# Attention kernel on one Trainium2 core: part of the exps moves from ScalarE to VectorE, under a new order of TensorE's queue

## The chip, the core and the metric

The kernel runs on one core of one Trainium2 chip. The metric is the device time of one execution in microseconds (us), the median of several runs. The engines are called as the profile calls them: PE is TensorE (matmuls; PEld its weight loads), ACT is ScalarE, DVE is VectorE, POOL is GpSimd, SP is SyncE, which issues DMAs.

## The reference

Two attentions over the same 2048 tokens of 512 features, mixed by a gate for each token:

```
g = sigmoid((x * gate_w).sum(-1))
a = A(x)    # 32 query heads of 16, one k and one v head that all of them share
b = B(x)    # 32 heads of 16, each with its own k and v
out = g * a + (1 - g) * b
# in both: p = softmax(q k^T / 4), o = p v, then o @ wo
```

There is no mask, so each of the 64 heads has 2048 x 2048 scores, and each score needs one exp.

## The kernel before, in words

The work is laid out as *groups*: 8 of them, attention A and B in turn, 8 heads each (`groups`). A group has two *halves* of 1024 queries; a half has four *banks*, each with 4 heads and 512 queries; a bank walks through 16 chunks of 128 keys. One chunk of one bank is a *quad*: 4 blocks of scores, 128 keys by 512 queries. So there are 64 banks of 16 quads. ACT takes two blocks at a time: one *exp* is one activation on 128 x 1024 scores, two exps make a quad, 32 exps a bank, 2048 exps the kernel.

For exp number `u`, `scores(u)` (matmuls L529, the exp L533) has PE write two blocks of scores into one of two PSUM tiles `sc`, as eight matmuls on 64 x 32 parts of the array. ACT reads them and writes the exps to one of six SBUF tiles `pr`. `values(m, half)` (L548) has PE multiply the exps of quad `m` with v, for 256 of the 512 queries; v carries a column of ones, so sums of exps come along. The results of a bank add up in one pair of PSUM banks `aux`; there are two such pairs. While one pair gathers a bank, the other (`spare()`) serves all else that PE does. At a bank's end `emptied` has DVE read the gathered pair (`raw`, L193 and L194), SP spreads it by DMAs to `dT` and `oT` (L570), and the pairs change their roles.

The rest of PE's work is *units*: the projections of q, k and v of the coming group (12 products each, L189), the turning of v (L416) and the output projections of the heads that are done (3 products, L189). A product is eight matmuls of 512 columns. When a unit's last product is out, DVE reads the spare pair (L193 and L194, or L450 for the output), and only then may the next unit write it. For q and k DVE also clips and splits the result (L356, L201, L202), and POOL's DMA queue lays it out for the scores (L338, eight DMAs to a move, a move at most every six exps). DVE's other work is *side* work: reciprocals (L462) and products (L469 to L471) of the softmax, and checks of the inputs' range (L198).

The program is recorded in order, in one loop over `u`, and each engine runs its instructions in that order. `_Tasks` holds the units and the side work. Its clock counts what PE has been given, in ns: `SCORES` 213 for the scores of an exp, `HALF` 428 for half a quad's values, `PRODUCT` 216 for a product, against `EXP` 916 for an exp of ACT; `busy` counts likewise for DVE. For each `u` the loop records the scores, one or two halves of values, products while they fit before the next exp, and side work while `busy` allows it.

Of the kernel before, what the change touches and what calls it, by code (L numbers as in the profile page):

```python
# [18 lines left out]
P = 128  # L19
# [3 lines left out]
DH = 16  # L23
# [8 lines left out]
FULL = 1500  # L32
LATE = 250
# [8 lines left out]
S_MAX = 40.0  # L42
RANGED = ["x", "gate", "wk_a", "wv_a", "wq_a", "wo_a", "wq_b", "wk_b", "wv_b", "wo_b", "v_a", "v_b"]
# [21 lines left out]
class _Tasks:  # L65
# [4 lines left out]
    def __init__(self):  # L70
        self.now, self.clock, self.busy, self.empty = 0, 0, 0, 0
        self.units, self.open, self.side = [], deque(), deque()
        self.moves, self.moved = deque(), 0

    def add(self, units, after, due, more=0):

        self.units += [(after, due, u, more) for u in units]
        self.units.sort(key=lambda u: u[1])
# [9 lines left out]
    def given(self, ns):  # L88
        self.busy = max(self.busy, self.clock + LATE) + ns

    def product(self, left):

        if not self.open:
            for u in self.units:
                if u[0] <= self.now and self.empty <= self.clock and len(u[2]) + 1 <= left:
                    self.units.remove(u)
                    self.open.extend(u[2])
                    self.more = u[3]
                    break
# [4 lines left out]
        if not self.open:  # L104
            self.given(FULL)
            self.empty = self.busy + LATE
            self.given(self.more)
        return True

    def late(self):  # L110

        n = len(self.open)
        for u in self.units:
            n += len(u[2]) + 3
# [12 lines left out]

    def flush(self):

        assert not self.moves  # L130
# [22 lines left out]
def _fast(ctx, tc, x, wq_a, wk_a, wv_a, wo_a, wqkv_b, wo_b, gate_w, out, flag):  # L153
    nc = tc.nc
    cst = ctx.enter_context(tc.tile_pool(name="cst", bufs=1))
    inp = ctx.enter_context(tc.tile_pool(name="inp", bufs=6))
    wts = ctx.enter_context(tc.tile_pool(name="wts", bufs=2))
    ops = ctx.enter_context(tc.tile_pool(name="ops", bufs=2))
    prob = ctx.enter_context(tc.tile_pool(name="prob", bufs=6))
    ps_s = ctx.enter_context(tc.tile_pool(name="ps_s", bufs=2, space=PSUM))  # L160
# [53 lines left out]
    weights, ready = {}, set()  # L214
    todo = _Tasks()

    def load_w(src, gi, queues=(nc.sync, nc.sync)):
# [4 lines left out]
        def one(part, at, bufs):  # L222
            w = inp.tile([P, BLK], F32, tag="in", name=f"w{part}{src}{gi}")
            w3 = w.rearrange("p (c m) -> p c m", c=NK)
            queues[part == "o"].dma_start(w if part == "o" else w3,
# [11 lines left out]
        if src == "a":  # L237
            one("q", wq_a[:, cols], 2)
            one("o", wo_a[cols, :], 3)
        else:  # L240
            for n, part in ((1, "k"), (2, "v"), (0, "q")):
                one(part, wqkv_b[:, n * D + gi * P : n * D + (gi + 1) * P], 2 if part == "q" else 1)
            one("o", wo_b[cols, :], 3)
# [5 lines left out]
    first_w = load_w("a", 0, (nc.scalar, nc.gpsimd))  # L249
# [40 lines left out]
    def kv_products(b, i, bank):  # L290
# [12 lines left out]
        kn = ops.tile([P, 4, 2, 4, DH], F16, tag="kn", name=f"kn{b}")  # L303
# [23 lines left out]
    def project(w, needs, name, kind, n0, half, parts, put, queues, late=None):  # L327
# [4 lines left out]
        def lay(p):  # L332
# [8 lines left out]
            ready.add((name, half, p))  # L341

        def product(i, c, a, b, first, last):
# [10 lines left out]
            y = ops.tile([P, BLK], F32, tag="y", name=f"y{name}{half}{i}")  # L354
# [36 lines left out]
    def v_units(gi):  # L391
# [3 lines left out]
        def product(b, n):  # L395
# [6 lines left out]
            y = ops.tile([P, BLK], F32, tag="y", name=f"yv{gi}{b}")  # L402
            v16 = ops.tile([P, 2, BLK], F16, tag="v16", name=f"v16{gi}{b}")
# [3 lines left out]
            todo.add([[lambda t=t: turned(b, v16, t) for t in range(4)]], todo.now + 4, todo.now, -400)  # L407

        def turned(b, v16, t):
# [15 lines left out]
            turns[gi] = turns.get(gi, 0) + 1  # L425
            if turns[gi] == 4:
                ready.add(("v", gi))
# [3 lines left out]
    turns = {}  # L431
# [24 lines left out]
    def norm_pieces(src, gi, half, t8, last):  # L456
# [7 lines left out]
        def parts():  # L464
            o, d = oT[src, gi, half, j][:, cols], dT[src, gi, half, j][:, cols]
            if t8 == 0:
                o16s[src, gi, half] = ops.tile([P, 2, 2 * BLK], F16, tag="o16", name=f"o16{src}{gi}{half}", bufs=3)
            o16 = o16s[src, gi, half][:, :, t8 * P : (t8 + 1) * P]
# [4 lines left out]
                     todo.now + (64 if last and half else 300))  # L473
# [44 lines left out]
    probs = {}  # L518

    def scores(u):  # L520
        todays = blocks[ACT * u : ACT * (u + 1)]
        sc = ps_s.tile([P, ACT, BLK], F32, tag="sc", name=f"sc{u}")
        for i, (n, half, _, c, p, j, hh) in enumerate(todays):
# [4 lines left out]
            for a in range(0, P, COLS):  # L528
                nc.tensor.matmul(sc[a : a + COLS, i], k[r, c * P + a : c * P + a + COLS],  # L529
# [290 lines left out]
```

## Time and profile before

| what | value |
|---|---|
| time, median of 3 runs (lowest to highest) | 1957.51 us (1956.01 to 1959.62) |
| the profiled execution's own time | 1959.14 us |
| its span, first to last instruction | 1956.9 us |
| mean granted clock of PE | 0.991 |
| busy: PE, ACT, DVE, POOL | 95%, 97%, 39%, 23% of the span |
| exps on ACT | 2048, from 28.4 us to 1927.2 us |

Busy shares are averages over the span. Instructions of ACT and of PE overlap with the next one, so the time that one takes is longer than the time from its start to the start of the next; where work is counted, the distance between starts is what matters. An idle stretch of an engine is put down to whatever released it last.

### The profile page before, as it was taken

What the parts mean: (1) busy time and instruction counts of PE and PEld (TensorE: products, weight loads), DVE (VectorE), ACT (ScalarE), POOL (GpSimd) and SP (SyncE); (2) the same over time, 40 slices, a digit from 0 to 9 for tenths busy, and PEclk for the clock granted to TensorE, in tenths of its full rate; (3) what the DMA queues carried; (4) which work ended last, traced back from release to release, by engine and by line L of the source; (5) the groups of instructions that cost most, each with busy time, mean ns of one, the idle gap of its engine ahead of it and who ended that gap; (6) DMA issues with size and microseconds to landing.
All of it is one profiled execution on the core that took longest, in us unless ns stands there. A gap on an engine that the chain in (4) does not pass through costs nothing.

```text
span 1956.9 us, 127404 instructions
## 1 busy us (share of the span) xinstructions
PE 1857.9 (95%) x59664; PEld 1060.7 (54%) x59664; DVE 756.9 (39%) x1429; ACT 1895.2 (97%) x2071; POOL 444.7 (23%) x840
## 2 busy tenths in 40 slices
PE   7999999999999999999999999999999999999995
PEld 4555655454555655555455655555455555555442
DVE  5344434343233344424234334443324334443432
ACT  4999999999999999999999999999999999999994
POOL 5344033230054031223034203302303502030000
PEclk8999999999999999999999999999999999999997
DMA  4121011110022010111012101100101201011101
GB/s 143 25 55 36 10 37 34 33 34 15 11 55 49 12 34 19 29 36 33 13 35 42 39 15 31 37 21 25 36 14 32 58 15 25 21 36 31 36 25 42
DMA packets 55736, 65.01 MB, mean 33 GB/s; under 512 B 21440, under 2 KB 29632, under 8 KB 55200
## 3 DMA queue, kind: packets, MB, share of 16 engines
q0 software_dynamic: 24112, 24.89, 6.4%
q1 hardware_dynamic: 30400, 31.46, 6.2%
q8 instruction: 469, 7.68, 1.7%
q14 instruction: 67, 0.55, 0.1%
q10 hardware_dynamic: 688, 0.43, 0.1%
HBM read 10.55 MB, written 4.19 MB: 8 GB/s over the span
## 4 chain that ended last, share of the span: by engine, by line
ACT 83%; issue 8%; PE 7%; DVE 2%; DMA 0%; SPq 0%; POOL 0%; ACTq 0%; DVEq 0%
ACT pr L533 82%; PE aux L548 3%; PE sc L529 2%; PE aux L189 2%; DVE xT L269 0%; DVE acc L450 0%; DMA acc<-in_A_x_dram 0%; PE aux L416 0%; ACT xT L268 0%; DVE dTb L462 0%; PE pt L264 0%; PE aux L297 0%; DMA dTb<-rawb 0%; PE aux L318 0%; PE aux L264 0%
## 5 line engine op out<-in xcount | busy, mean ns | idle before, releaser
L533 ACT ACTIVATE pr<-sc 128x1024 f32<-128x1024 f32 x2048 | 1884.6, 1191 | 12.6 <-PE sc L529 11.7
L548 PE MATMUL aux<-pr,vA 64*32 64x256 f32 x16384 | 685.3, 377 | 2.3 <-issue 1.9
L548 PE MATMUL aux<-pr,vB 64*32 64x256 f32 x16384 | 646.7, 376 | 0.1
L529 PE MATMUL sc<-Qa,kA 64*32 64x512 f16 x8192 | 453.4, 384 | 18.4 <-issue 0.3
L529 PE MATMUL sc<-Qb,K 64*32 64x512 f16 x8192 | 424.1, 385 | 41.8
L529 PEld LDWEIGHTS <-K 64*32 64x32 f16 x8192 | 209.3, 89 | 387.5 <-issue 309.0
L548 PEld LDWEIGHTS aux<-pr,vA 64*32 64x32 f32 x16384 | 335.7, 105 | 58.0 <-issue 15.1
L529 PEld LDWEIGHTS <-kA 64*32 64x32 f16 x8192 | 209.7, 90 | 277.3 <-issue 207.3
L548 PEld LDWEIGHTS aux<-pr,vB 64*32 64x32 f32 x16384 | 309.7, 105 | 35.4 <-issue 0.7
L450 DVE SCALAR_TENSOR_TENSOR acc<-aux,gate_up,acc 128x512 f32<-128x512 f32 x240 | 180.2, 751 | 326.6 <-PE aux L189 312.9
L338 POOL DMA_DIRECT2D Qa<-hia x118 | 57.8, 489 | 449.4 <-PE sc L529 299.1
L338 POOL DMA_DIRECT2D Qb<-hib x128 | 62.3, 486 | 359.5 <-DVE hib L201 181.7
L189 PE MATMUL aux<-w16ob,o16b 64*32 64x512 f16 x1536 | 80.3, 391 | 15.1 <-ACT o16b L470 13.2
L189 PE MATMUL aux<-xT,w16vb 64*32 64x512 f16 x1536 | 93.8, 376 | 0.1
L193 DVE TENSOR_SCALAR rawb<-aux 128x512 f32<-128x512 f32 x32 | 22.1, 689 | 179.9 <-PE aux L548 179.7
L338 POOL DMA_DIRECT2D K<-hik x128 | 61.5, 485 | 109.3 <-DVE hik L201 102.4
L189 PE MATMUL aux<-xT,w16kb 64*32 64x512 f16 x1536 | 82.2, 376 | 0.0
L189 PE MATMUL aux<-xT,w16qb 64*32 64x512 f16 x1536 | 79.9, 376 | 0.0
L189 PE MATMUL aux<-xT,w16qa 64*32 64x512 f16 x1536 | 79.5, 376 | 0.4 <-DVE xT L269 0.2
L189 PE MATMUL aux<-w16oa,o16a 64*32 64x512 f16 x1536 | 79.3, 376 | 0.0
L462 DVE RECIPROCAL dTa<-dTa 128x128 f32<-128x128 f32 x64 | 55.6, 918 | 59.8 <-DMA dTa<-rawa 59.8
L462 DVE RECIPROCAL dTb<-dTb 128x128 f32<-128x128 f32 x64 | 55.4, 916 | 52.9 <-DMA dTb<-rawb 52.9
(135 smaller groups left out, 991.2 us busy)
## 6 DMA issues: line engine op xcount, KB each, us to landing
acc<-in_A_x_dram SPq DMA_DIRECT2D x16, 256.0 KB, 5.9
dTa<-rawa SPq DMA_DIRECT2D x128, 32.0 KB, 2.6
oTa<-rawa SPq DMA_DIRECT2D x128, 32.0 KB, 3.2
K<-hik POOLq DMA_DIRECT2D x128, 32.0 KB, 2.7
K<-lok POOLq DMA_DIRECT2D x128, 32.0 KB, 2.9
Qb<-hib POOLq DMA_DIRECT2D x128, 32.0 KB, 2.5
Qb<-lob POOLq DMA_DIRECT2D x128, 32.0 KB, 2.8
out_dram<-acc SPq DMA_DIRECT2D x16, 256.0 KB, 2.6
```

The costliest lines, as they stand in the source:

```text
L189: nc.tensor.matmul(out[n : n + COLS], lhsT[r, n : n + COLS], rhs[r], start=start, stop=stop)
L193: nc.vector.tensor_scalar(dst, outs[0], scale, None, op0=ALU.mult)
L338: queues[(8 * p + n) % len(queues)].dma_start(op[to : to + DH].rearrange("d (a q) -> d a q", a=2), state[part][rows])
L450: nc.vector.scalar_tensor_tensor(acc[:, t], bank, g, acc[:, t], op0=ALU.mult, op1=ALU.add)
L462: nc.vector.reciprocal(d, d)
L529: nc.tensor.matmul(sc[a : a + COLS, i], k[r, c * P + a : c * P + a + COLS], Q[src, gi, half, p][r, j * BLK : (j + 1) * BLK], start=True, s ...
L533: nc.scalar.activation(probs[u][:, :m], sc[:, :m], AF.Exp, scale=SCALE / (UP * UP))
L548: nc.tensor.matmul(o[32 * i : 32 * i + 32, cols], v[r], probs[at // ACT][r, at % ACT, cols], start=c == half == 0, stop=c == NT - 1 and ha ...
```

## The change

1. **Two exps of some quads are made by DVE.** `choose` may take the last quad of the bank after the one being worked on, if the quad that is being reached is among the first seven of its bank (`LATEST`), the fourth bank has begun, DVE's backlog is short and k and q have been laid. Its two pairs of blocks are left out of ACT's row. Instead each becomes a unit of PE: `vector_scores` writes the scores to the spare `aux` pair. DVE then makes the exps with nine instructions: two that read PSUM and write the score, scaled by 2^23/ln 2 and shifted, as int32; two bitwise ones that part the 23 low bits (as a float near one) from the exponent's bits; and five multiply-adds of a polynomial in the first part, the last of which multiplies with the second, a power of two. All but the first two work on 128 x 1024 in SBUF. The last seven are `fill`: `beside` records them one by one where DVE is expected to have time.
2. **The order follows PE's time.** `slip` and `max(..., todo.clock)` let the planned clock run over an exp's 916 ns, by up to `OVER` 160 before products stop; values of the two kinds of quads are taken as they are expected to be ready; values are recorded without scores between them while more than six exps wait for theirs. So products now come in another pattern: two after one exp and one after the next, where before there was one after each.
3. **Dates and tiles.** v's four units have dates of their own, output units are due before the end (`ends_by`), output weights are loaded later, and `emptied` records all side work that is due (`hurry`) ahead of a bank's reading. To make room, the pool for weights has 3 tiles instead of 6, and `y`, `v16`, `oT` and `dT` one instead of two.

The first rows on ACT around the last quad of bank 34, before; `pr` and `sc` carry the number of the exp:

```order
L533 ACTIVATE pr1116_29253<-sc1116_29244 128x1024
L533 ACTIVATE pr1117_29280<-sc1117_29271 128x1024
L533 ACTIVATE pr1118_29310<-sc1118_29301 128x1024
L533 ACTIVATE pr1119_29352<-sc1119_29343 128x1024
L533 ACTIVATE pr1120_29371<-sc1120_29362 128x1024
```

And the same place in the changed kernel:

```order
L569 ACTIVATE pr1116_29501<-sc1116_29492 128x1024
L569 ACTIVATE pr1117_29520<-sc1117_29511 128x1024
L569 ACTIVATE pr1120_29539<-sc1120_29530 128x1024
L569 ACTIVATE pr1121_29558<-sc1121_29549 128x1024
L569 ACTIVATE pr1122_29588<-sc1122_29579 128x1024
```

Exps 1118 and 1119 are gone from ACT's queue. In the whole program 1974 rows of this kind are left of 2048: 74 exps, the last quads of 37 banks, have moved.

DVE before, where the second q unit for the later half of this group is read (`ya`), and then the bank (`raw`):

```order
L193 TENSOR_SCALAR ya_27583<-aux_82 128x512
L194 SCALAR_TENSOR_TENSOR ya_27583<-aux_83,ya_27583 128x512
L356 TENSOR_SCALAR ya_27583<-ya_27583 128x512
L201 TENSOR_SCALAR hia_26894<-ya_27583 128x512
L202 SCALAR_TENSOR_TENSOR loa_26895<-ya_27583,hia_26894 128x512
L198 TENSOR_REDUCE stats<-ya_27583 128x1
L193 TENSOR_SCALAR rawa_27675<-aux_84 128x512
L194 SCALAR_TENSOR_TENSOR rawa_27675<-aux_85,rawa_27675 128x512
```

DVE in the changed kernel, from the last row of that unit on; `vpr` are the exps that DVE makes, `part` the two bit parts:

```order
L234 TENSOR_REDUCE stats<-ya_28309 128x1
L581 TENSOR_SCALAR vpr_28398<-aux_85 128x512
L581 TENSOR_SCALAR vpr_28398<-aux_86 128x512
L587 TENSOR_SCALAR part_28458<-vpr_28398 128x1024
L587 TENSOR_SCALAR part_28460<-vpr_28398 128x1024
L581 TENSOR_SCALAR vpr_28498<-aux_85 128x512
L581 TENSOR_SCALAR vpr_28498<-aux_86 128x512
L592 SCALAR_TENSOR_TENSOR vpr_28398<-part_28458 128x1024
L485 SCALAR_TENSOR_TENSOR acc<-aux_85,gate_up,acc 128x512
L485 SCALAR_TENSOR_TENSOR acc<-aux_86,gate_up,acc 128x512
L592 SCALAR_TENSOR_TENSOR vpr_28398<-vpr_28398,part_28458 128x1024 x3
L229 TENSOR_SCALAR rawa_28736<-aux_87 128x512
```

Between the unit and the bank's reading now stand the work for two exps, in part, and the reading of an output unit (`acc`); the polynomial of exp 1118 (`vpr_28398`) is cut in pieces by the readings, and three of its steps stand right ahead of the bank's.

PE in the changed kernel, at the scores of exp 1118, between the values of exps 1070 and 1071 and the next scores for ACT:

```order
L613 MATMUL aux10_87<-pr1071_28291,vA_95 32x256
L613 MATMUL aux11_88<-pr1071_28291,vA_95 32x256
L562 LDWEIGHTS kA_94
L562 MATMUL aux00_85<-Qa200_24708,kA_94 32x512
L562 LDWEIGHTS kA_94
L562 MATMUL aux00_85<-Qa200_24708,kA_94 32x512
```

These scores go to an `aux` pair and stand where a product could stand, some 44 exps ahead of their old place; before, all scores went to `sc`.

The core of the diff:

```diff
+NARROW = 710
+LATEST = 6
+WIDE = 1240
+OVER = 160
...
     def given(self, ns):
         self.busy = max(self.busy, self.clock + LATE) + ns
+    def beyond(self, ns):
+        self.busy = max(self.busy, self.begun) + ns
...
-    def beside(self, until):
+    def beside(self, until, urgent):
+        limit = until + (len(self.open) * EXP + 600 if self.open else 1400)
+        def filled():
+            while self.fill and self.busy <= until + EXP and max(self.busy, self.begun) + self.fill[0][1] <= limit:
+                f, ns = self.fill.popleft()
+                f()
+                self.beyond(ns)
+        if urgent:
+            filled()
         while self.side and self.side[0][0] <= self.now and self.busy <= until:
             _, f, ns = self.side.popleft()
             f()
-            self.given(ns)
+            self.beyond(ns)
+        filled()
...
-    inp = ctx.enter_context(tc.tile_pool(name="inp", bufs=6))
+    inp = ctx.enter_context(tc.tile_pool(name="inp", bufs=3))
+    vec = ctx.enter_context(tc.tile_pool(name="vec", bufs=1))
...
+    def vector_scores(u):
+        sc = spare()
+        products(u, sc)
+        asked.remove(u)
+        held[0] += 1
+        probs[u] = pr = vec.tile([P, ACT, BLK], F32, tag="pr", name=f"vpr{u}", bufs=3)
+        fix = pr.bitcast(I32)
+        for i in range(ACT):
+            nc.vector.tensor_scalar(fix[:, i], sc[i], SCALE / (UP * UP) / math.log(2) * 2.0 ** 23, -(2.0 ** 23),
+                                    op0=ALU.mult, op1=ALU.add)
+        parts = []
+        def part(a, b, op):
+            t = vec.tile([P, ACT, BLK], I32, tag=f"part{len(parts)}", name=f"part{len(parts)}{u}")
+            nc.vector.tensor_scalar(t, fix, a, b, op0=ALU.bitwise_and, op1=op)
+            parts.append(t.bitcast(F32))
+        def horner(i):
+            m, power = parts
+            nc.vector.scalar_tensor_tensor(pr, pr if i < 4 else m, VEC[i], m if i else power, op0=ALU.add, op1=ALU.mult)
+            if i == 0 and u % 2:
+                taken[u // 2] = max(todo.busy, todo.begun) + WIDE + LATE
+        todo.fill.append((lambda: part(0x7FFFFF, 125 << 23, ALU.bitwise_or), NARROW))
+        todo.fill.append((lambda: part(0x7F800000, 0x40000000 | VEC5, ALU.bitwise_xor), NARROW))
+        todo.fill.extend((lambda i=i: horner(i), WIDE) for i in range(4, -1, -1))
...
+        todo.hurry()
         raw = ops.tile([P, BLK], F32, tag="raw", name=f"raw{src}{gi}{half}{s}", bufs=1)
...
     def half_values(u):
-        m, half = divmod(done, 2)
-        if done == halves or 2 * m + 1 > u - 2:
-            return False
+        if half_done:
+            m = half_done[0]
+        elif waits and waits[0][0] // NT == done // (2 * NT) and waits[0][1] <= u - 2:
+            m = waits[0][0]
...
+        else:
+            m = next((m for m in pending if in_time(m)), None)
+            if m is None:
+                return False
...
+    def choose(now, m):
+        if asked or len(todo.fill) > 1 or todo.busy > todo.clock + 1500 or todo.late() or m < 3 * NT:
+            return
+        if sum(ns for after, _, ns in todo.side if after <= now) > 2000:
+            return
+        q = m - m % NT + 2 * NT - 1
+        if q >= len(blocks) // 4 or q in vector or m % NT > LATEST:
+            return
...
+        vector.add(q)
+        pending.append(q)
+        for u in (2 * q, 2 * q + 1):
+            asked.append(u)
+            todo.add([[lambda u=u: vector_scores(u)]], now, now + 8, 0, 2 * 700, lambda: held[0] < 3)
...
     while done < halves:
         u += 1
-        todo.now, todo.clock = u, u * EXP
+        while u - acts_done > 6 and at < len(blocks) // 4:
+            slip += EXP
+            todo.begun = todo.clock = max(u * EXP + slip, todo.clock)
+            if not half_values(u):
+                todo.product(left())
+            todo.beside(todo.clock + EXP, True)
+        todo.now, todo.clock = u, max(u * EXP + slip, todo.clock)
+        todo.begun, end = todo.clock, (u + 1) * EXP + slip
...
-        if half_values(u) and done < u - 2 and u % 2:
+        if half_values(u) and (u - acts_done > 2 or any(map(in_time, pending))) and todo.clock + HALF <= end + OVER:
             half_values(u)
-        if todo.late() and u % 2:
-            end += PRODUCT
-        while todo.clock + PRODUCT <= end and todo.product(-done % (2 * NT)):
+        while todo.clock + PRODUCT <= end + OVER and todo.product(left()):
             pass
```

More of the change, by code (lines that the diff above doesn't have):

```diff
@@ L126, in beside, with hurry @@
             self.moves.popleft()()
+    def hurry(self):
+        while self.side and self.side[0][0] <= self.now:
+            _, f, ns = self.side.popleft()
+            f()
+            self.beyond(ns)
     def flush(self):
[L130 removed]
+        assert not self.moves and not self.fill
         ahead = 0
@@ L517, in _fast, with products @@
               for s, bank in enumerate(banks) for c in range(NT) for p, j, hh in bank]
[L518 to L523, printed above, removed]
+    probs, vector, taken, later = {}, set(), {}, []
+    def products(u, sc):
+        for i, (n, half, _, c, p, j, hh) in enumerate(blocks[ACT * u : ACT * (u + 1)]):
             src, gi = groups[n]
```

168 lines of the change are left out of this document (110 added, 58 removed).

## The prediction

> **What bounds the kernel now.** The page was read first: busy times, then the chain.
>
> ```profile
> PE 1857.9 (95%) x59664; PEld 1060.7 (54%) x59664; DVE 756.9 (39%) x1429; ACT 1895.2 (97%) x2071; POOL 444.7 (23%) x840
> PEclk8999999999999999999999999999999999999997
> ACT 83%; issue 8%; PE 7%; DVE 2%; DMA 0%; SPq 0%; POOL 0%; ACTq 0%; DVEq 0%
> L533 ACT ACTIVATE pr<-sc 128x1024 f32<-128x1024 f32 x2048 | 1884.6, 1191 | 12.6 <-PE sc L529 11.7
> ```
>
> Two engines look full. The third row decides between them: over 2048 exps ACT waited 12.6 us, nearly all for scores from PE. So ACT bounds the kernel, and what matters is the distance from one exp to the next. A stretch of ACT's timeline without a gap gives it:
>
> ```profile
> 299.49 31.47 ACT L533 ACTIVATE pr<-sc 128x1024 f32<-128x1024 f32 x34
> ```
>
> An exp lasts 1.19 us on the average (row above) but overlaps with the next: (31.47 - 1.24) / 33 = 0.916 us from start to start, 1.24 being the last one's own length (the median that the view of the tile sc gives):
>
> ```profile
> L533 ACT ACTIVATE pr<-sc x2048: 1017/1242/1250, 28.4 to 1926.0; 128x1024 f32<-128x1024 f32 x187
> ```
>
> 2048 x 0.916 = 1876 us, of 1899 from the first exp to the end of the last. The rest is the start and waits. The waits of ACT from 60 to 1925 us are one row:
>
> ```profile
> ACT pr L533 <- PE sc L529: 6.0, 17, 0.8
> ```
>
> PE's 95% is not what it needs, since a waiting matmul's modelled end counts as busy. Its need shows where it runs without waiting for ACT:
>
> ```profile
> 1088.80 0.51 PE L189 MATMUL aux<-xT,w16vb 64*32 64x512 f16 x8
> 1089.01 0.51 PE L529 MATMUL sc<-Qa,kA 64*32 64x512 f16 x8
> 1089.23 0.73 PE L548 MATMUL aux<-pr,vA 64*32 64x256 f32 x16
> 1089.66 0.73 PE L189 MATMUL aux<-xT,w16vb 64*32 64x512 f16 x16
> 1090.09 0.51 PE L529 MATMUL sc<-Qa,kA 64*32 64x512 f16 x8
> ```
>
> From start to start: a product 0.21 to 0.215 (two took 0.43), the scores of an exp 0.22, half a quad's values 0.43. There are 9216 / 8 = 1152 products. So PE needs 2048 x (0.216 + 0.43) + 1152 x 0.216 = 1572 us, and some 10 us for the turning of v and the rest: 84% of ACT's 1876. The clock row above shows 0.9 or more of PE's clock granted in all but the first and the last slice. DVE, at 39%, has some 1200 us free.
>
> **Part 1, exps taken from ACT.** 74 exps leave ACT's queue (1974 of 2048 stay): 74 x 0.916 = 67.8 us. ACT is the bound nearly all the way, so this comes off the span whole as long as PE still hands over scores in time: 1956.9 - 67.8 = 1889.1 us.
>
> **The same exps on DVE.** Per exp: two readings of PSUM, two bitwise instructions and five multiply-adds on 128 x 1024. Nearest rows:
>
> ```profile
> L193 DVE TENSOR_SCALAR yk<-aux 128x512 f32<-128x512 f32 x16 | 11.1, 692 | 115.1 <-PE aux L189 115.1
> L202 DVE SCALAR_TENSOR_TENSOR lok<-yk,hik 128x512 f16<-128x512 f32 x16 | 11.1, 692 | 0.6
> L469 DVE SCALAR_TENSOR_TENSOR oTb<-oTb,dTb 128x128 f32<-128x128 f32 x64 | 17.5, 275 | 0.8 <-DMA oTb<-rawb 0.8
> L201 DVE TENSOR_SCALAR hib<-yb 128x512 f16<-128x512 f32 x16 | 6.8, 427 | 0.5
> L470 DVE CAST o16b<-oTb 128x128 f16<-128x128 f32 x60 | 13.6, 227 | 2.1
> ```
>
> The PSUM readings are the first row, 0.69 each. A multiply-add on 512 columns takes 0.692, on 128 it takes 0.275: 384 columns cost 0.417, so 1024 cost 0.692 + 512/384 x 0.417 = 1.25. An instruction with one SBUF input takes 0.427 and 0.227: 1024 cost 0.427 + 512/384 x 0.200 = 0.69. Whether a bitwise one on int32 goes at that rate no row shows. Its bounds are 0.69 and the 1.25 of the two-input row; I take 0.69, as its shape (one SBUF input, a constant) is that of L201. Together 2 x 0.69 + 2 x 0.69 + 5 x 1.25 = 9.0 us an exp, 74 x 9.0 = 666 us (at the other bound 10.1 and 749). DVE then has 757 + 666 = 1423 us of work in some 1890, 75% (at most 80%): hidden as a total, but not everywhere. The heaviest stretch from one bank's reading to the next, counted from the order with these durations, holds about 31 us of DVE work, and a bank with 30 exps lasts 27.5 us; its neighbours hold 20 and 22, so a backlog of some 3 us arises and goes again. What waits for DVE then is PE, whenever its next unit needs the `aux` pair that DVE has yet to read; and behind PE, ACT.
>
> **The order of PE.** PE's work is unchanged in amount: the scores move to `aux` at the same 0.216. Only its pattern changes. Per bank in the order, the fullest needs 93.5% of ACT's time (before: 92%). Finer: of stretches of eight exps, 46 of 241 need over 97% of ACT's time, before 10 of 250; of stretches of four none needs over 100%, before 10 did, by up to 6%. One exp followed by two products needs 0.216 + 0.43 + 0.43 = 1.08 us, 0.16 more than ACT takes. ACT has an exp in hand for that: PE may start scores when the exp before the last ends and has 0.916 - 0.216 = 0.7 us to finish them, some 0.5 with the handover seen here as slack. The lone excess of 0.16 fits. What doesn't fit is PE halting by itself, as it did in before, in its tightest place:
>
> ```profile
> 1093.12 0.79 PE L548 MATMUL aux<-pr,vA 64*32 64x256 f32 x16
> 1093.55 1.31 PE L189 MATMUL aux<-xT,w16vb 64*32 64x512 f16 x16
> 1094.49 0.58 PE L529 MATMUL sc<-Qa,kA 64*32 64x512 f16 x8
> ...
> 1095.17 1.02 ACT L533 ACTIVATE pr<-sc 128x1024 f32<-128x1024 f32 x1 [0.49 <-PE sc L529]
> ```
>
> Two products took 0.94 us there instead of 0.43, and ACT lost 0.49. So the estimate for new waits: before's 6.0 us fell in its 10 tight stretches, 0.6 each; 46 of them would give 28 us, 22 more than now. The other end is no more than now, as no stretch is over full any longer; even a gain of up to 6.0, if today's waits go with the order that made them, can't be excluded. Between -6 and +22 I take +12: more places where a halt shows, none where the order itself is at fault, and DVE's backlog beside it. Span: 1889.1 + 12 = 1901.
>
> **Start and end.** The rows before the first exp are the same. At the end the same 12 products and readings in the same order follow the last exp:
>
> ```profile
> 1925.63 2.69 PE L548 MATMUL aux<-pr,vB 64*32 64x256 f32 x64
> 1928.36 0.69 DVE L193 TENSOR_SCALAR rawb<-aux 128x512 f32<-128x512 f32 x1 [17.64 <-PE aux L548]
> 1937.05 1.06 PE L189 MATMUL aux<-w16ob,o16b 64*32 64x512 f16 x16 [8.73 <-ACT o16b L470]
> 1950.18 1.60 DVE L450 SCALAR_TENSOR_TENSOR acc<-aux,gate_up,acc 128x512 f32<-128x512 f32 x2 [1.59 <-PE aux L189]
> ```
>
> The 30 us from 1927.2 on stay, so 0.
>
> **Dates and tiles** cost nothing if their cover holds. Three weight tiles are enough while a load comes long after its tile's last reader: loads are a half-group, some 112 us, apart. Single `oT` and `dT` hold back only SP's DMAs of the next pair of banks, and side work that is due is recorded ahead of them. A bank's reading now stands behind that side work and behind polynomial steps; who waits is PE's next unit on that pair. The price of that cover being gone is the second and third rival.
>
> **POOL** shares time with DVE somewhere: one of 48 clips took longer.
>
> ```profile
> L356 DVE TENSOR_SCALAR yk<-yk x16: 426/427/508, 97.7 to 1543.4; 128x512 f32<-128x512 f32 x16
> L338 POOL DMA_DIRECT2D K<-hik x128 | 61.5, 485 | 109.3 <-DVE hik L201 102.4 <-DMA K<-hik 4.0 <-issue 2.8
> L205 POOL TENSOR_SCALAR wqb<-wqb 128x512 f32<-128x512 f32 x4 | 6.0, 1488 | 0.3
> ```
>
> By these, 0.08 us in one case of 48, and I add nothing. The Trainium skill (page "SBUF — State Buffer", section "Who interferes with whom") speaks against the change here: a one-input DVE instruction at double rate takes the pair of ports that POOL needs, for its whole length, and a two-input one blocks those POOL instructions that read SBUF; whoever comes second waits to the end. By that rule the sum would be the same until POOL's laying of k and q is late, which is the fourth rival.
>
> **The numbers.** The profiled execution took 1959.1 us, 2.2 over its span, and lies 1.6 over the median of 1957.5. So 1901 + 2.2 - 1.6 = 1902 us, 2.8% less than before.
>
> **Rivals.**
>
> *Forecast, 0.75:* ACT stays the bound and new waits are -6 to +25 us: 1884 to 1915, likeliest 1902.
>
> *PE becomes a second bound, 0.15.* Tight stretches, halts and DVE's backlog add up, as ACT's hand of 0.5 us is used up and comes back by only 0.05 us an exp (0.916 - 0.862 with one product each). For it: PE's need rises from 84% of ACT's time to 87% (1582 of 1808), and DVE's from 39% to 75%. Against it: in before PE caught up within a few exps. Price: about 1 us for each of 37 quads beyond the 12: 1939 at most, likeliest 1925.
>
> *DVE's readings come late, slower than before, 0.07.* In the order a bank's reading can stand behind three polynomial steps, 3 x 1.25 = 3.7 us that nothing interrupts, and PE's queue is strictly in order: if PE's next unit is already on that pair, its scores for ACT stand behind it. After 0.5 us ACT starves: 3.2 us for each of 37 quads is 118 us, 1889 + 118 = 2007, 2008 as a time. The change turns into a loss from 67.8 / 37 = 1.83 us a quad on. For it: the bitwise instructions may take 1.25, and then DVE's real time runs 1.1 us an exp behind the planned one. Against it: the order places no unit on a pair before DVE is expected to have read it.
>
> *POOL lays k and q late, no change, 0.03.* A move is eight issues, 8 x 0.485 = 3.9 us, in a slot of 6 x 0.916 = 5.5. Were each issue held up to 1.1 us by DVE, a move would take 8.8, and four moves 13 us longer than four slots; a q unit that is done only when due, 24 exps ahead, would be laid 13 us late. Most are done earlier, so I take 4 us at the start of each of 14 halves: 1902 + 56 = 1958. It decides only from 0.69 us an issue on.
>
> That the exps don't leave ACT isn't possible by the order: its rows are gone.
>
> **How the range and chances follow.** The forecast's own ends are 1884 and 1915; its low end needs all of today's waits to go, so the range begins at 1888. It reaches to 1935 for most of the second rival, which leaves out the third and fourth (0.10) and the tails of the first two. 0.2% is 4 us, about what a measurement here can tell from no change. Faster by more: 0.75 + 0.15 + a little of the fourth = 0.91; within: 0.02; slower: 0.07.
>
> **What would show it.** ACT's group should have 1974 exps, still 0.916 apart in a gapless stretch, with about 18 us of waits for PE; DVE busy near 1420 us; bitwise instructions of 0.69 us and multiply-adds of 1.25; PE's busy share up. The forecast is wrong if ACT's waits exceed 40 us: PE waiting for DVE in its rows speaks for the third case, PE without waits for the second, POOL's issues over 0.7 us for the fourth.

## The result and the profile after

| | before | changed |
|---|---|---|
| time, median (lowest to highest) | 1956.76 us (1955.45 to 1959.62) | 1910.74 us (1907.04 to 1914.90) |
| ratio, 95% interval | 1 | 0.9765 [0.9752, 0.9778] |
| the profiled execution, its span | 1959.1 us, 1956.9 us | 1907.7 us, 1905.9 us |
| exps on ACT | 2048, 28.4 to 1927.2 us | 1974, 29.3 to 1876.5 us |

The time of before is here over four runs, one more than ahead of the prediction. The change is worth 2.35%; the forecast was 1902 us, 2.8%. The two profiled executions lie 51 us apart, the medians 46: the one of the changed kernel is 3.0 us below its median and the one of before 2.4 above. The page of the changed kernel, its busy times, the start of its chain and its costliest group (busy us, mean ns of one, idle before and what ended it):

```profile
PE 1800.7 (94%) x59664; PEld 1124.5 (59%) x59664; DVE 1382.3 (73%) x2095; ACT 1831.9 (96%) x1997; POOL 466.3 (24%) x840
ACT 67%; PE 15%; issue 12%; DVE 4%; DMA 1%; SPq 0%; DVEq 0%; ACTq 0%; POOL 0%
L569 ACT ACTIVATE pr<-sc 128x1024 f32<-128x1024 f32 x1974 | 1821.3, 1090 | 24.7 <-PE sc L562 21.1
```

ACT is still the fullest engine, but its share of the chain went from 83% to 67% and PE's from 7% to 15%: the chain now runs through PE more often. The busy time of DVE nearly doubled. The longest stretch of ACT's timeline without a gap that the view shows gives the rate of an exp again:

```profile
1203.94 174.45 ACT L569 ACTIVATE pr<-sc 128x1024 f32<-128x1024 f32 x190 [0.46 <-PE sc L562]
```

(174.45 - 1.09) / 189 = 0.917 us from one to the next, 1.09 being the mean length of one. The rate is that of before, although the mean length in the group's row fell from 1191 to 1090 ns. The waits of ACT from 60 to 1880 us:

```profile
ACT pr L569 <- PE sc L562: 16.1, 32, 4.5
ACT pr L569 <- PE aux L613: 1.0, 1, 1.0
```

6.0 us became 17.1. This view shows only waits in which ACT stood idle. A fuller count is the distance from the end of one exp to the end of the next, less 0.9165 us, added up over all exps from 60 us on; it is called *lost time* below. It is 13.1 us in before and 30.2 us in the changed kernel: 56 and 98 losses of over 0.05 us, 6 and 12 of them over 0.5 us. So the span's account is -67.8 (74 exps) + 17.1 (lost time) - 0.3 (what follows the last exp, 29.7 and 29.4 us) = -51.0, as measured. The first exp starts 0.9 us later, but at 60 us all but 0.1 us of that is made up.

One wait of 4.48 us stands out. DVE and PE in the timeline around it:

```profile
1812.28 8.86 DVE L234 TENSOR_REDUCE stats<-xT 128x1 f32<-128x2048 f16 x4
1821.36 0.69 DVE L229 TENSOR_SCALAR rawb<-aux 128x512 f32<-128x512 f32 x1
...
1827.93 1.77 DVE L497 RECIPROCAL dTb<-dTb 128x128 f32<-128x128 f32 x2 [5.08 <-DMA dTb<-rawb]
1829.61 1.51 DVE L485 SCALAR_TENSOR_TENSOR acc<-aux,gate_up,acc 128x512 f32<-128x512 f32 x2
1830.32 0.58 PE L225 MATMUL aux<-w16oa,o16a 64*32 64x512 f16 x1 [2.96 <-DVE acc L485]
...
1832.78 1.02 ACT L569 ACTIVATE pr<-sc 128x1024 f32<-128x1024 f32 x1 [4.48 <-PE sc L562]
```

Four reductions of the range check hold DVE for 9 us, from 1812.28 on, so the bank's reading (`rawb`) starts only at 1821.36, the DMAs that spread it land late, the reciprocals wait 5.08 us for them at the head of DVE's queue, the reading of an output unit (`acc`) stands behind the reciprocals, PE's next product waits for that reading, and the scores for ACT stand behind the product. That is the third rival's chain, but the work in front is the range check and not the polynomial.

Behind PE's waits for DVE are 8.3 of the 30.2 us lost (counted in the 4 us that follow each of its 10 waits of over 0.15 us), 4.6 of them at this one exp; in before PE waits for DVE nowhere between 60 us and the last exp.

The instructions that DVE took on, and POOL's issues with their shortest, median and longest duration:

```profile
L581 DVE TENSOR_SCALAR vpr<-aux 128x512 int32<-128x512 f32 x148 | 95.2, 685 | 36.8 <-PE aux L562 36.2
L587 DVE TENSOR_SCALAR part<-vpr 128x1024 int32<-128x1024 int32 x148 | 103.1, 728 | 0.7
L592 DVE SCALAR_TENSOR_TENSOR vpr<-vpr,part 128x1024 f32<-128x1024 f32 x296 | 363.5, 1228 | 6.1
L592 DVE SCALAR_TENSOR_TENSOR vpr<-part 128x1024 f32<-128x1024 f32 x74 | 90.3, 1221 | 1.6
```

```profile
L587 DVE TENSOR_SCALAR part<-vpr x148: 682/687/1654, 127.0 to 1784.6; 128x1024 int32<-128x1024 int32 x148
L375 POOL DMA_DIRECT2D K<-lok x128: 484/484/1007, 112.8 to 1540.0; - x128
```

### The profile page after: what moved, and what is told of

Its sections match the earlier page's. It is cut to its first block, busy times and chain, and to the rows that moved or that the text cites. A ratio compares the mean times of both kernels' runs of the same rounds, so it can differ in the third digit from the quotient of the medians.

```text
span 1905.9 us, 128055 instructions
## 1 busy us (share of the span) xinstructions
PE 1800.7 (94%) x59664; PEld 1124.5 (59%) x59664; DVE 1382.3 (73%) x2095; ACT 1831.9 (96%) x1997; POOL 466.3 (24%) x840
## 4 chain that ended last, share of the span: by engine, by line
ACT 67%; PE 15%; issue 12%; DVE 4%; DMA 1%; SPq 0%; DVEq 0%; ACTq 0%; POOL 0%
ACT pr L569 67%; PE aux L613 7%; PE sc L562 4%; PE aux L225 4%; DVE stats L234 1%; DVE acc L485 0%; DVE vpr L592 0%; DMA acc<-in_A_x_dram 0%; DVE dTb L497 0%; DMA dTb<-rawb 0%; PE aux L300 0%; DVE v L238 0%; DVE yv L230 0%; DVE yv L229 0%; DVE xT L305 0%
## 5 line engine op out<-in xcount | busy, mean ns | idle before, releaser
L569 ACT ACTIVATE pr<-sc 128x1024 f32<-128x1024 f32 x1974 | 1821.3, 1090 | 24.7 <-PE sc L562 21.1
L613 PE MATMUL aux<-pr,vA 64*32 64x256 f32 x15712 | 647.2, 376 | 2.0 <-issue 1.8
L613 PE MATMUL aux<-pr,vB 64*32 64x256 f32 x15872 | 636.4, 376 | 0.6 <-issue 0.4
L562 PE MATMUL sc<-Qa,kA 64*32 64x512 f16 x7856 | 441.2, 380 | 28.0 <-ACT pr L569 4.7
L592 DVE SCALAR_TENSOR_TENSOR vpr<-vpr,part 128x1024 f32<-128x1024 f32 x296 | 363.5, 1228 | 6.1
L613 PEld LDWEIGHTS aux<-pr,vA 64*32 64x32 f32 x15712 | 328.6, 105 | 57.8 <-issue 9.8
L581 DVE TENSOR_SCALAR vpr<-aux 128x512 int32<-128x512 f32 x148 | 95.2, 685 | 36.8 <-PE aux L562 36.2
L587 DVE TENSOR_SCALAR part<-vpr 128x1024 int32<-128x1024 int32 x148 | 103.1, 728 | 0.7
L592 DVE SCALAR_TENSOR_TENSOR vpr<-part 128x1024 f32<-128x1024 f32 x74 | 90.3, 1221 | 1.6
L225 PE MATMUL aux<-w16ob,o16b 64*32 64x512 f16 x1536 | 70.4, 391 | 16.0 <-ACT o16b L505 13.3
```

The costliest lines, as they stand in the source:

```text
L225: nc.tensor.matmul(out[n : n + COLS], lhsT[r, n : n + COLS], rhs[r], start=start, stop=stop)
L562: nc.tensor.matmul(sc[i][a : a + COLS], k[r, c * P + a : c * P + a + COLS], Q[src, gi, half, p][r, j * BLK : (j + 1) * BLK], start=True, s ...
L569: nc.scalar.activation(probs[u], sc, AF.Exp, scale=SCALE / (UP * UP))
L581: nc.vector.tensor_scalar(fix[:, i], sc[i], SCALE / (UP * UP) / math.log(2) * 2.0 ** 23, -(2.0 ** 23), op0=ALU.mult, op1=ALU.add)
L587: nc.vector.tensor_scalar(t, fix, a, b, op0=ALU.bitwise_and, op1=op)
L592: nc.vector.scalar_tensor_tensor(pr, pr if i < 4 else m, VEC[i], m if i else power, op0=ALU.add, op1=ALU.mult)
```

## The experiments

The chips differ a little, so each ratio is against before on the same chip: 1964.7 us for the first four, 1962.5 for the next four, 1965.7 for the last three. Lost time is of one profiled execution of each kernel, and before was profiled on the first chip only (13.1 us), so a few us between two lost times say little. In the counts of intervals below, PE's work between the scores of one ACT exp and the next is added up from the order with the durations of the prediction; scores, half a quad's values and two products need 0.216 + 0.43 + 0.43 = 1.08 us, scores and a whole quad's values as much, and an interval over 1.0 us is called *long*. Before has 45 long intervals, the changed kernel 345.

**The order without the exps.** `choose` never takes a quad; 2048 exps stay on ACT, in the new order.

```diff
     def choose(now, m):
-        if asked or len(todo.fill) > 1 or todo.busy > todo.clock + 1500 or todo.late() or m < 3 * NT:
-            return
+        return
```

> The new order and dates with no exp moved: all 2048 exps stay on ScalarE. Theory (the gain is the exps taken from ScalarE, 74 x 0.9165 = 67.8 us, less new waits): 1952 to 1970 us, with 10 to 25 us of ScalarE's time lost after 60 us against 13 of before; no gain. Rival (the new order itself brings a good part of the gain): under 1945 us.

Measured: 1983.1 us, ratio 1.0098 [1.0083, 1.0114], lost time 32.3 us. The page's group and ACT's waits:

```profile
L569 ACT ACTIVATE pr<-sc 128x1024 f32<-128x1024 f32 x2048 | 1890.2, 1109 | 26.3 <-PE sc L562 23.8
ACT pr L569 <- PE sc L562: 18.0, 41, 0.8
```

The order by itself costs 0.0098 x 1964.7 = 19 us, about as much as the changed kernel's new waits, and with DVE no fuller than before (757 us busy in both). That is more than was expected, in time and in lost time, and it moves most of the cause away from DVE's new work.

**No polynomial.** The scores still go to `aux` and DVE still reads them; the seven instructions behind the two readings go. PE's and ACT's orders are those of the changed kernel.

```diff
-            nc.vector.tensor_scalar(fix[:, i], sc[i], SCALE / (UP * UP) / math.log(2) * 2.0 ** 23, -(2.0 ** 23),
+            nc.vector.tensor_scalar(fix[:, i], sc[i], SCALE / (UP * UP) / math.log(2) * 2.0 ** 23, 127 * 2.0 ** 23,
...
         def part(a, b, op):
-            t = vec.tile([P, ACT, BLK], I32, tag=f"part{len(parts)}", name=f"part{len(parts)}{u}")
-            nc.vector.tensor_scalar(t, fix, a, b, op0=ALU.bitwise_and, op1=op)
-            parts.append(t.bitcast(F32))
+            pass
...
-            m, power = parts
-            nc.vector.scalar_tensor_tensor(pr, pr if i < 4 else m, VEC[i], m if i else power, op0=ALU.add, op1=ALU.mult)
```

> Leaves out the two bitwise instructions and the five multiply-adds: an exp on VectorE is then the two readings of PSUM alone, which make a piecewise linear exp. The orders of TensorE and ScalarE are the changed kernel's. Theory (most of the 30 us that ScalarE now loses are TensorE halting by itself in a fuller queue, a few long ones come from VectorE): 1903 to 1908 us, lost time 20 to 27 us. Rival (VectorE's backlog makes the new losses): 1890 to 1898 us, lost time 10 to 15 us.

Measured: 1921.2 us, 0.9777 [0.9760, 0.9795], lost time 43.9 us. Its busy times and ACT's waits:

```profile
PE 1812.4 (94%) x59664; PEld 1129.9 (59%) x59664; DVE 846.2 (44%) x1577; ACT 1836.6 (96%) x1997; POOL 445.8 (23%) x840
ACT pr L569 <- PE sc L562: 24.3, 58, 4.7
```

536 us of DVE's busy time are gone and nothing is won: the lost time is even above what either theory or rival allowed. So the polynomial's backlog on DVE does not make the new waits. The wait behind the range check, 4.7 us, is there too; that one is DVE's, but not the polynomial's.

**The range check in pieces.** The 9 us of reductions become four tasks, 4 exps apart. A limit on the quads, the last two lines, keeps the same 74 exps moved.

```diff
-                todo.add_side([flag_stats], now + 60, [9000])
-                todo.add_side([flag_reduce], now + 75, [400])
-                todo.add_side([flag_check], now + 90, [1500])
+                for c in range(NK):
+                    todo.add_side([lambda c=c: x_stats(c)], now + 67 + 4 * c, [2300])
+                todo.add_side([small_stats], now + 83, [1000])
+                todo.add_side([flag_reduce], now + 86, [400])
+                todo.add_side([flag_check], now + 95, [1500])
...
-        if q >= len(blocks) // 4 or q in vector or m % NT > LATEST:
+        if q >= 62 * NT or q in vector or m % NT > LATEST:
```

> The range checks of x at the end (four reductions of 2.28 us, recorded as one piece) are spread over the last two banks as pieces of their own; the same 74 exps on VectorE. Theory (the longest wait of ScalarE, 4.5 us at 1832 us, comes from a bank's reading behind this piece): 1904 to 1907 us, 4 to 6 less than the changed kernel, and no wait over 2 us in the last 80 us. Rival (the wait there comes from the output units' dates or single tiles, not from the piece): no difference.

Measured: 1915.1 us, 0.9742 [0.9725, 0.9760], lost time 40.8 us. The longest wait fell from 4.5 to 1.1 us, so its chain is shown. The lost time as a whole is not lower (30.2 and 36.5 us in two executions of the changed kernel), so the gain of the whole kernel is not:

```profile
ACT pr L569 <- PE sc L562: 20.0, 52, 1.1
```

**More work in each polynomial.** The first multiply-add is issued three times, 2 x 2 x 1.22 = 4.9 us more DVE work for a quad. The planner does not know of it.

```diff
-            nc.vector.scalar_tensor_tensor(pr, pr if i < 4 else m, VEC[i], m if i else power, op0=ALU.add, op1=ALU.mult)
+            for _ in range(3 if i == 4 else 1):
+                nc.vector.scalar_tensor_tensor(pr, pr if i < 4 else m, VEC[i], m if i else power, op0=ALU.add, op1=ALU.mult)
```

> The first multiply-add of each exp on VectorE is made three times (2 x 1.23 us more, 182 us in all, VectorE busy 82%); the planner does not know. Theory (VectorE's readings come late only at a few places): +5 to +25 us, 1915 to 1936. Rival (the third rival of the prediction, readings late at every quad): over 3 us for each of 37 quads, 1957 us or more, no gain left.

Measured: 2035.5 us, 1.0360 [1.0337, 1.0384], lost time 161.9 us. The waits from 60 to 1880 us, and one place in the timeline:

```profile
ACT pr L569 <- PE sc L562: 128.4, 112, 4.5
PE aux L225 <- DVE acc L485: 19.6, 30, 1.2
PE aux L225 <- DVE yb L229: 12.8, 8, 2.4
PE aux L225 <- DVE yk L229: 10.1, 4, 3.0
```

```profile
420.22 3.74 DVE L593 SCALAR_TENSOR_TENSOR vpr<-part 128x1024 f32<-128x1024 f32 x3
423.88 0.68 DVE L229 TENSOR_SCALAR ya<-aux 128x512 f32<-128x512 f32 x1
424.62 0.37 PE L225 MATMUL aux<-xT,w16qa 64*32 64x512 f16 x1 [2.80 <-DVE ya L229]
...
426.78 1.02 ACT L569 ACTIVATE pr<-sc 128x1024 f32<-128x1024 f32 x1 [4.03 <-PE sc L562]
```

Three steps of 1.22 us stand ahead of a reading, PE waits 2.80 us for it, ACT 4.03 us for its scores. This place is the third rival's chain, with the polynomial in front. Counted from 60 us to the last exp, PE waits 112 times for DVE, 86.6 us in all, against 10 times and 7.5 us in the changed kernel, and 124.4 of the 161.9 us are lost in the 4 us behind these waits. Against the changed kernel (0.9765 and 0.9785 in its two runs, 1919 to 1922 us on this chip) it costs 113 to 117 us, 3.1 us for each of 37 quads, and turns the gain into a loss, at a DVE that is 76% busy. PE's granted clock was 0.978 to 0.982 in these runs, about 0.01 below the others; no run tells why. My theory (5 to 25 us) failed here: 4.9 us a quad that the planner does not know of are more than the cover over DVE's readings. That the same steps would be covered if the planner knew of them was not run.

**The order with one product to an interval.** As the first experiment, and products stop where the exp's time ends. No interval is long.

```diff
-OVER = 160
+OVER = 0
```

> As the run of the new order alone (all 2048 exps on ScalarE), with OVER = 0: no interval between two exps holds more TensorE work than ScalarE takes, one product at most after each exp. Theory (the new order costs because intervals of 1.08 us use up ScalarE's one exp in hand, so that TensorE's own halts show): as the kernel before, 0.995 to 1.003 of its time, lost time under 20 us. Rival (the dates, the single tiles or the side work ahead of a bank's reading cost): 1.007 to 1.012, as the order alone.

Measured: 1956.3 us, 0.9973 [0.9962, 0.9984], lost time 8.0 us. Group and waits:

```profile
L569 ACT ACTIVATE pr<-sc 128x1024 f32<-128x1024 f32 x2048 | 1882.6, 1187 | 9.8 <-PE sc L562 8.8
ACT pr L569 <- PE sc L562: 3.0, 10, 0.5
```

The 1% is gone, so it belongs to the allowance `OVER`; the rest of the order, with its dates, single tiles and `hurry`, costs nothing (before, 0.3% slower, has 45 long intervals). How a long interval costs is seen in two places of the same work, qb's products, where PE halts for about 0.55 us each time. First the order alone (the halt is the break before 1137.70, in matmuls that should follow at once):

```profile
1134.42 3.83 ACT L569 ACTIVATE pr<-sc 128x1024 f32<-128x1024 f32 x4
...
1135.50 0.52 PE L562 MATMUL sc<-Qa,kA 64*32 64x512 f16 x8
1135.71 0.74 PE L613 MATMUL aux<-pr,vA 64*32 64x256 f32 x16
1136.14 0.74 PE L225 MATMUL aux<-xT,w16qb 64*32 64x512 f16 x16
1136.58 0.53 PE L562 MATMUL sc<-Qa,kA 64*32 64x512 f16 x8
1136.79 0.73 PE L613 MATMUL aux<-pr,vA 64*32 64x256 f32 x12
1137.70 0.41 PE L613 MATMUL aux<-pr,vA 64*32 64x256 f32 x2 [0.18 <-issue]
...
1138.85 2.85 ACT L569 ACTIVATE pr<-sc 128x1024 f32<-128x1024 f32 x3 [0.60 <-PE sc L562]
```

And the order with one product to an interval:

```profile
1139.95 0.48 PE L562 MATMUL sc<-Qa,kA 64*32 64x512 f16 x8
1140.17 0.70 PE L613 MATMUL aux<-pr,vA 64*32 64x256 f32 x16
1140.60 0.48 PE L225 MATMUL aux<-xT,w16qb 64*32 64x512 f16 x8
1140.87 0.43 PE L562 MATMUL sc<-Qa,kA 64*32 64x512 f16 x8
1141.09 0.37 PE L613 MATMUL aux<-pr,vA 64*32 64x256 f32 x1
1141.63 0.45 PE L613 MATMUL aux<-pr,vA 64*32 64x256 f32 x8 [0.17 <-issue]
...
1142.85 2.86 ACT L569 ACTIVATE pr<-sc 128x1024 f32<-128x1024 f32 x3 [0.20 <-PE sc L562]
```

With two products (x16) the scores before the halt start 1.08 us after those before them (1135.50 to 1136.58), and ACT's reserve is spent when the halt comes: it waits 0.60 us. With one (x8) they start 0.92 us apart, and the same halt costs 0.20 us.

The same was counted over the traces from 60 us to the last exp, with a halt as over 0.25 us from the start of one matmul to the next of the same line and tiles, where the next has no semaphore to wait for. The order alone has 42 halts, and ACT loses 20.5 of its 32.3 us in the 4 us behind them; with one product to an interval it is 22 halts and 5.3 of 8.0 us. So 15.2 of the 24.3 us between the two lie behind halts, for two reasons: a halt costs twice as much, 0.49 against 0.24 us, and twice as many show. The first is what the theory said, and the other traces agree: 0.27 us a halt in before, with 45 long intervals, and 0.40 to 0.47 in the nine others with 220 and more, the run with longer polynomials left out. Why more halts show in the fuller order is not known; the count also differs between two executions of one kernel (34 and 54 in the changed one). Nor is the single long interval told apart from the tight stretch of the prediction: of some 245 stretches of eight exps, those that need over 97% of ACT's time go too, from 7 to 52 (by the exp at which the eights begin) to 1 at most.

**Half of the exps.** Every third bank only, 38 exps moved instead of 74; 337 long intervals.

```diff
         q = m - m % NT + 2 * NT - 1
+        if q // NT % 3:
+            return
```

> Only every third bank may give its last quad to VectorE: 38 exps moved instead of 74. Theory (the order costs about 1% whatever is moved, and each exp moved gives its 0.9165 us): 1.0098 - 38 x 0.9165 / 1960 = 0.992, 0.990 to 0.994. Rival (each exp moved brings its own waits, so that gain goes with their number from no change at none): half of the gain, 0.988 or less.

Measured: 1948.3 us, 0.9928 [0.9915, 0.9942], lost time 38.1 us. With 0, 38 and 74 exps moved the ratio is 1.0098, 0.9928 and 0.9785 (below). If each exp gives 0.9165 us of 1963, the order's own cost comes out as 1.0098, 0.9928 + 0.0177 = 1.0105 and 0.9785 + 0.0345 = 1.0130: nearly fixed, while each exp gives close to its full price. The first 0.9765 would give 1.0110 in place of the last.

**The changed kernel again**, on the chip of the last two and the next.

> The changed kernel as it is, on the chip of these runs: 0.975 to 0.978 of the kernel before, 25 to 45 us lost, as TensorE's halts differ from run to run.

Measured: 1919.0 us, 0.9785 [0.9767, 0.9804], a little above what was expected; lost time 36.5 us, its longest wait 4.4 us.

**The range check in pieces, as the planner then likes it:** as above, without the limit to the same quads, which gives 76 exps.

> The range checks of x spread over the last banks, and the 38 quads that the planner then chooses (76 exps). Theory: 4.5 us less for the long wait and 1.8 us for two exps, 0.971 to 0.975 of the kernel before, below the changed kernel of these runs. Rival (other work of VectorE waits in its place): as the changed kernel.

Measured: 1915.5 us, 0.9757 [0.9743, 0.9770], just outside what was expected. It is below the changed kernel on the same chip by 3.5 us if the medians are taken and by 5.5 if the ratios are, with intervals that overlap a little; the wait that is gone was of that size. On a third chip it was run once more:

> The version with the range check in pieces and 76 exps moved, on the chip of these two, as their measure: ratio 0.975 to 0.977, ScalarE's lost time 36 to 42 us, no single wait over 1.5 us.

Measured: 1918.6 us, 0.9759 [0.9738, 0.9780], lost time 42.0 us. The three runs with the check in pieces (0.9742, 0.9757, 0.9759) lie below the two without (0.9765, 0.9785). It is the best version here, by some 0.2%, which is not clear of noise.

**Fewer long intervals, with exps moved.** The version with the check in pieces, but a pair of products is allowed only while a product is overdue.

```diff
-        while todo.clock + PRODUCT <= end + OVER and todo.product(left()):
+        while todo.clock + PRODUCT <= end + (OVER if todo.late() else 0) and todo.product(left()):
```

> The version with the range check in pieces, but two products follow one exp only while a product is overdue: the order then moves 56 exps instead of 76, and 227 intervals between exps need over 1.0 us of TensorE instead of 347. If the long intervals set the cost of the order (ratio 1.0098 with 306 of them, 0.9973 with none), 227 of them cost about 0.9973 + 227/306 x 0.0125 = 1.0066, and 56 exps give 56 x 0.9165 = 51.3 us or 0.026: ratio 0.980, ScalarE's lost time some 6 to 10 us less than in the version with 76 exps on the same chip. Rival: the cost hangs on how full longer stretches are, not on the count of long intervals; then it stays near 1.0098 and the ratio is 0.984, with the same lost time as 76 exps.

Measured: 1933.7 us, 0.9836 [0.9821, 0.9850], lost time 39.5 us. The number is the rival's, but the reason is another, so the run does not decide. A wait that was nearly absent has come in:

```profile
ACT pr L569 <- PE sc L562: 15.5, 41, 1.1
ACT pr L569 <- PE aux L613: 8.7, 10, 1.0
```

In four stretches PE has put the values off so far that ACT runs out of `pr` tiles, as I read the second row, and waits for them; these stretches lose some 12.5 of the 39.5 us. The remaining 27 against 42.0 in the version with 347 long intervals would fit a cost by long intervals, but that is worked out afterwards.

**More exps.** The version with the check in pieces; the planner is told that an exp takes longer and finds place for 86; 457 long intervals, and some stretches of eight exps that need up to 1.058 of ACT's time.

```diff
-EXP = 916
+EXP = 975
```

> The version with the range check in pieces, planned with 0.975 us for an exp instead of 0.916, so that the order finds place for 86 exps, with 457 long intervals instead of 347 and a few stretches of eight exps that need up to 1.058 of ScalarE's time. If each exp is worth its 0.9165 us and each long interval some 0.08 us (24.5 us by 306), ten exps more give 9.2 us and 110 long intervals take 8.8: the same time as with 76 exps within 4 us. Rival: TensorE is now so full that the over-full stretches add up, at about 1 us for each of 43 quads: 30 us or more slower than with 76 exps.

Measured: 1926.8 us, 0.9796 [0.9780, 0.9812], lost time 57.5 us, 277 losses against 149. Ten more exps give 9.2 us and the lost time takes 15.5: 8 us slower than 76 exps on the same chip. The theory was 4 us too kind and the rival, at 30 us or more, far off. Placed in this way, more exps bring nothing; since `EXP` shifts all dates, the run does not show that no other order could hold them.

## Why the prediction was right, and where it was off

**Exps taken from ACT: right.** 74 x 0.916 = 67.8 us. The distance in a stretch without gaps is 0.917 us again, and over 38 and 74 exps the time follows that price to within 0.3% of the whole, which is 6 of 68 us.

**The same exps on DVE: right in kind, a little large.** The four rows add up to 95.2 + 103.1 + 363.5 + 90.3 = 652 us, 8.8 an exp, against 9.0 and 666. The bitwise instructions took 0.687 us in the median, the end that I took, and the multiply-adds 1.224 instead of 1.25. DVE's busy time is 1382 us instead of 1423, because overlapping instructions count once in it: their durations add up to 1455 us.

**The order of PE: the term that was mis-sized.** The prediction put it at +12 us of new waits, between -6 and +22, "none where the order itself is at fault, and DVE's backlog beside it". Measured are +17.1 us of lost time between the two profiled executions. By the medians it is more: 67.8 us taken from ACT and 46.0 gained leave 21.8, the range's very end, and on the second chip 67.8 and 43.5 leave 24.3, beyond it. Of the 8.7 us by which 1902 was too low, 4.9 are in the span; most of the rest is that the profiled execution lies 3.0 under its median, where the prediction set it 1.6 over.

The order alone, without any backlog, costs 19 us. The sentence on the fault was wrong: "The lone excess of 0.16 fits" holds for an exp by itself, but the order has 345 such intervals, and each leaves ACT's reserve of 0.5 us so small that a halt of PE, for which the prediction had a quoted case, is passed on to ACT. Taking that allowance out took the cost out of the order alone. For the changed kernel itself this is argued and not shown, since no run has 74 exps moved without long intervals. What its trace shows is that 15.7 of the 30.2 us are lost behind 34 halts, in before 8.5 of 13.1 behind 31. The upper end of the range, 0.6 us for each of 46 tight stretches, was reckoned from this effect, and whether such stretches or the single long intervals count, no run separates: the one with fewer long intervals has fewer tight stretches as well (17 to 28 against 39 to 50 in the changed kernel). That the polynomial's backlog on DVE is no part of it is shown, as nothing was won with 536 us less on DVE. But DVE's queue has a part: the range check ahead of a bank's reading made 4.6 of the 17.1 us, and the prediction named only polynomial steps there.

**ACT's waits in the view: 17.1 us**, close to the 18 that I named as a sign, partly by luck. The view leaves out the small losses in which an exp only starts later behind its predecessor; by the ends of exps the loss is 30.2 us. PE's busy share did not rise as I had said but fell from 95% to 94%. It counts the time in which matmuls wait as well, so it does not follow PE's work; that they wait less for ACT now would fit, but was not counted.

**The second rival** (PE as a second bound, 1925) points to the right engine, and the changed kernel lies between the forecast and it. With 86 exps, ten more brought a loss; with 74 the exps still gave nearly their full price.

**The third rival** (DVE's readings late, 2008) did not happen in the changed kernel, apart from the single wait of 4.48 us. The experiment with 4.9 us more for a quad shows that its mechanism is real, and that it is near: it sets in when the polynomial takes a few microseconds more than the planner was told. That its price of 3.2 us a quad was met (3.1 measured) is in part luck: the loss came in 112 waits of PE of 0.8 us in the mean, and not in 37 losses of 3.2.

**The fourth rival** (POOL late): its issues took 488 to 514 ns in the mean against 485 to 489, far from 690, and the longest rose to 1007 ns. The Trainium skill (page "SBUF — State Buffer", section "Who interferes with whom") says that DVE instructions at double rate and POOL shut each other out for a whole instruction; the trace agrees in kind, with single bitwise instructions of 1654 instead of 687 ns and POOL's issues of up to twice 484. Each of the three longest bitwise instructions (1652 to 1654 ns) starts 0.38 us after an instruction of POOL and ends 0.55 us behind that one's end. PE waited nowhere for a transfer of k or q.

**Start and end: right.** 29.7 us followed the last exp in before, 29.4 now.

What stays open is why PE halts within a group of matmuls that wait for nothing. Most halts begin 1.5 to 2.5 us after a DMA of the instruction queue starts: 28 of the 31 in before, 21 of 34 in the changed kernel, 36 of 42 in the order alone, where chance would give a quarter. That speaks for the supply of PE's instructions, but no run here changed that supply, so it is only argued.

## What to carry to other kernels

When work leaves the bounding engine, the next thing to ask is how much room the engine that feeds it still has in each single interval, and not on the average: an order that fills some intervals to 118% and others to less cost nothing by its own arithmetic, and 1% here, where the feeder stumbles now and then. An exp taken from the bound was worth its distance to the next one, nearly in full; the cost of the order that makes the move possible was nearly fixed (1.0 to 1.3%), so measure the order alone as well. And where a queue is strictly in order, the margin ahead of a reading has to be known in microseconds: here 4.9 us more for a quad, unknown to the planner, turned a gain of over 2% into a loss of 3.6%.

## What the runs showed of the hardware

- The reported length of an activation is not its cost. Before has a mean of 1191 ns, the order alone 1109 ns with the same exps and a longer time; in gapless stretches the ends are 0.917 us apart in both kernels. Behind a wait the starts come 0.903 us apart and the reported length grows by 13.5 ns an exp up to 1.24 us: so I read it as holding time in which an exp that has started waits for the one before it.
- A bitwise instruction with a constant on int32, 128 x 1024, takes 0.687 us in the median, as much as was estimated for a one-input instruction on float32 from the rows of before (0.69), and 56% of what as many columns take with two inputs (1.224).
- PE halts by itself: over 0.25 us from one matmul to the next of the same line and tiles, without a semaphore, 31 times for 13.3 us in before and 34 times for 14.8 us in the changed kernel, up to 0.98 us; in the order alone 42 times, up to 1.43 us.
